# Backward of a recurrent-memory transformer on one core: the three projections of dH summed in one PSUM bank, in pairs of heads with 256 weight columns

## The chip, the cores and the metric

The kernel runs on one core of one Trainium2 chip. The metric is the device time of one execution in microseconds; three executions of the kernel before gave 3080.75, 3083.49 and 3086.59 us, median 3083.49. A core has a matrix engine (TensorE, "PE" in the profile, its weight loads "PEld"), a vector engine (DVE), a scalar engine (ACT), GpSimd (POOL), a queue engine (SP), and 16 DMA engines. PE reads two operands from SBUF, a stationary one (the weights in the array, loaded ahead) and a moving one that streams through, and writes PSUM, which has eight banks of 128 partitions by 512 float32 here. DVE and ACT bring results from PSUM to SBUF.

## What is computed

The reference is a block of adaLN conditioning, attention with a recurrent memory, and a gated feed-forward, with all its gradients. What matters here is the attention's backward pass. The forward pass goes over 64 segments of 32 tokens in order; each sees 8 memory rows and its own rows, and its first 8 output rows are the next segment's memory:

```python
h = jnp.concatenate([mem, xs], axis=1)          # (1, 8 + 32, 512)
q = jnp.einsum('btd,dhe->bhte', h, Wq)          # 32 heads of 128
k = jnp.einsum('btd,dhe->bhte', h, Wk)
v = jnp.einsum('btd,dhe->bhte', h, Wv)
...
o = jnp.einsum('bhte,hed->btd', o, Wo)
mem = o[:, :M, :].copy()
```

Backward therefore goes over the segments from the last to the first, and each one needs the gradient of its first 8 output rows from the one before it. That gradient is part of dH, the gradient of `h`:

dH = sum over heads of (dQ_h Wq_h^T + dK_h Wk_h^T + dV_h Wv_h^T),

a sum of 96 products of a 40x128 by a 128x512 matrix per segment. The 32 columns that hold the memory rows and the first 24 tokens are computed inside the loop; the last 8 tokens of each segment (its tail) are gathered over four segments and computed as one set of 32.

## The kernel before, in words

`phase4` is the backward loop, `for s in reversed(range(NS))` (L1560) with NS = 64. Its instructions are pinned on every engine in the order in which the Python code issues them (`self.pin(i0)`, L1755), so the code's order is each engine's order. Per segment it takes the gradient of the output rows, `dyT`, through Wo (`col_pass`, tile `pass_ps`), turns it per head (`turn`), and makes dV, dP, dS, dK and dQ in three parts of 12, 12 and 8 heads (`grad_mm`, `grad_out`, `dp`, `ds`, `dstt`). The gradients come out as `dVT`, `dKT` and `dQT`, with the head's 128 channels on the partitions and 32 columns for the rows of each head.

**The dH products.** With `X` (one of the three gradients) as the stationary operand, 128 by 32, a product fills 32 of the array's 128 columns. Four such products stand side by side in four column strips (`tile_position=(0, 32 * j)`) and write 32 partitions of the bank each.

- `dht` (L1641) does dV and dK with `col_mm` (L212): head n goes to strip n % 4, with all 512 weight columns moving. Each strip sums a quarter of the heads, so the bank `dh_ps`, 128 by 512, holds four partial sums of the whole 32x512 result. dV's first 24 heads come early (L1686, L1687), while the scores' gradient is made on DVE; dK's 32 heads and dV's last 8 come at L1722 to L1724.
- `dht_pairs` (L1649) does dQ with `pair_mm` (L218): two heads at a time, four products. Strips 0 and 1 take weight columns 0 to 255 of the two heads, strips 2 and 3 columns 256 to 511 of the same two. The bank `dhq_ps`, 128 by 256, holds two partial sums of each half.

**The split and the fold.** The partial sums are added on PE, by products with 0/1 matrices. To lose no precision in bf16, a bank is split in two parts, `hi` (ACT, a copy in bf16) and `lo` (DVE, bank less `hi`). `fold_split` (L307) does it for `dh_ps`, 128 by 512, into the tile of `dST`; `split_pair` (L226) for `dhq_ps`, 128 by 256, into `dh_hi` and `dh_lo`. `fold_sum` (L316) then makes 16 products of 32 columns into one bank `dh_ft`: eight with `foldsel` (adds four strips) on the first split, eight with `foldhalf` (adds two strips) on the second. `sum_pair` (L235), with the eight of the second kind alone, is what forward uses for its output projection.

**What lies around it.** Between the end of the dQ products and the fold stand, on PE, a piece of the tail's products (`tail.chunk()`, L1728; the pieces have 16, 24, 8, 8, 16, 8 and 16 products of 512 columns and are handed out over four segments) and, once in four segments, the tail's own fold (`self.pop_later()`, L1730, tile `dh_b_ft`). After the fold ACT brings the first 8 columns of `dh_ft` into the next segment's `dyT` (L1734), and PE goes on with a pass for the tails, `proj_b` (L1483), a turn of it, or another tail piece, and then with the next segment's `col_pass` on `dyT`.

**PSUM.** `psp` has six banks that are handed out in turn (tag "p": `pass_ps`, `turn_ps`, `g_ps`, `dp_ps`, `dhq_ps`, `dh_ft` and so on). `psb` has one bank for the tail (tag "b") and one, tag "dh", that `dh_ps` and `proj_b`'s `pass_ps` share.

**Queues.** SP issues the loads of the saved forward tiles and the two transposing DMAs of dK and dQ; POOL issues the stores, copies `dOst` and gathers the tails.

Of the kernel before, what the change touches and what calls it, by code (L numbers as in the profile page):

```python
# [8 lines left out]
F32 = mybir.dt.float32  # L9
# [31 lines left out]
class K:  # L41
# [1356 lines left out]
    def phase4(self):  # L1398
        nc, tc, cfg, io = self.nc, self.tc, self.cfg, self.io
        D, DC, H, E, L, M, T, G, NS = cfg.D, cfg.DC, cfg.H, cfg.E, cfg.L, cfg.M, cfg.T, cfg.G, cfg.NS  # L1400
        GW = 128
# [4 lines left out]
        with self.p4_ctx as ctx:  # L1406
            WqT, WkT, WvT, WoT, negones = self.WqT, self.WkT, self.WvT, self.WoT, self.negones
# [4 lines left out]
            sb2 = ctx.enter_context(tc.tile_pool(name="p4s2", bufs=2, reuse_waits="tile"))  # L1412
            psp = ctx.enter_context(tc.tile_pool(name="p4ps", bufs=6, space=PSUM, reuse_waits="tile"))
            psb = ctx.enter_context(tc.tile_pool(name="p4psb", bufs=1, space=PSUM, reuse_waits="tile"))
            NP = 3
            PG = 4
# [136 lines left out]
            def store_rows_x(left):  # L1553
                while len(row_stores) > left:
                    row_stores.pop(0)()
# [4 lines left out]
            for s in reversed(range(NS)):  # L1560
# [12 lines left out]
                dS, dST, dOst = dSs[0], dSTs[0], dOst_t  # L1573
                dVT, dKT, dQT = dXTs["dVT"][0], dXTs["dKT"][0], dXTs["dQT"][0]
# [63 lines left out]
                dh_ps = [None]  # L1638
                n_dh = [0]

                def dht(X, WT, pi):  # L1641
                    if dh_ps[0] is None:
                        dh_ps[0] = psb.tile([128, 512], F32, name="dh_ps", tag="dh")
                    for h in range(pi * PG * 3, min(H, (pi + 1) * PG * 3)):
                        off = (h // 3) * GW + (h % 3) * 32
                        self.col_mm(dh_ps[0], X[:, off:off + 32], WT[:, h, :], n_dh[0], 2 * H)
                        n_dh[0] += 1

                def dht_pairs(X, WT):  # L1649
                    ps = psp.tile([128, 256], F32, name="dhq_ps", tag="p")  # L1650
                    off = lambda h: (h // 3) * GW + (h % 3) * 32
                    for n in range(H // 2):
                        hs = (2 * n, 2 * n + 1)
                        self.pair_mm(ps, [X[:, off(h):off(h) + 32] for h in hs], [WT[:, h, :] for h in hs], n, H // 2)
                    return ps

                for a, n, eng in ((0, 4, "dve"), (4, 2, "act"), (6, 2, "act")):
                    self.col_pass(psp, WoT, 0, lambda c: dyT[:, c, :], RAd, eng, steps=(a, n))
# [25 lines left out]
                ds(2)  # L1684
                self.pop_later()
                dht(dVT, WvT, 0)  # L1686
                dht(dVT, WvT, 1)  # L1687
                gv2 = grad_mm("dVT", dOst, Pst, 2)
                gr0 = grad_mm("dV", Pst, dOst, 0)
# [32 lines left out]
                for pi in range(NP):  # L1722
                    dht(dKT, WkT, pi)
                dht(dVT, WvT, 2)  # L1724
                parts = self.fold_split(sb2, dh_ps[0], "dh", dST)
                pair = self.split_pair(sb2, dht_pairs(dQT, WqT), "dh")
                tail.collect(s % nseg_t, [dVT, dKT, dQT])
                tail.chunk()  # L1728
                if split:
                    self.pop_later()  # L1730
                store_rows_x(2)
                ft = self.fold_sum(psp, parts, "dh", "p", pair)
                if dyT_next is not None:
                    nc.scalar.activation(dyT_next[:, :, 0:M], ft[:, :, 0:M], AF.Copy)  # L1734
                g = s // 4
# [428 lines left out]
```

## Time and profile before

| | |
|---|---|
| median of three executions | 3083.49 us (3080.75 to 3086.59) |
| the profiled execution, its own time | 3080.64 us |
| its span, first to last instruction | 3078.9 us |
| PE busy | 2985.9 us, 97% |
| DVE, ACT, POOL busy | 1613.0, 1254.4, 1386.1 us |
| mean granted PE clock | 0.991 |
| first and last `dhq_ps` product | 1546.7 and 2501.3 us |

How to read the lines: a group is "line engine operation out<-in shapes xcount | busy us, mean ns of one | idle time before it". Busy time of a group is a union, so products that overlap are counted once. A line number can be a helper's: L215 is `col_mm`, L223 `pair_mm`, L255 `col_pass`, L323 `fold_sum`, L240 `sum_pair`. In a timeline a line starts with the moment and the duration of a run of equal instructions. A matmul's end is modelled, and the next one starts long before it, so the distance from one line's start to the next line's is what a run costs. A bracket at the end of a line names an idle time of the engine and who ended it. In the list of waits the three numbers are the total in us, how often, and the longest.

### The profile page before, as it was taken

Reading aid. Unit: us, or ns where it says so; the run is one execution under the profiler, and the core shown is the slowest. Engines: PE = TensorE matmul, PEld = TensorE weight load, DVE = VectorE, ACT = ScalarE, POOL = GpSimd, SP = SyncE. Lnnn points to the kernel's source line nnn. Section 1 sums busy time; section 2 is a strip of 40 time slices with the busy share of each in tenths; the row PEclk is TensorE's granted clock in tenths of the full one; section 3 lists DMA queues with packets and bytes.
Section 4 is the critical chain, followed back from the end, with each engine's and each line's share of the span. In section 5 each row is a group of like instructions: output and inputs, shape, how many; then the busy total and the mean of one; then the engine's idle time right before and its main releaser. Section 6 shows DMA issues by size and latency. Waiting matters only on the chain.

```text
span 3078.9 us, 106050 instructions
## 1 busy us (share of the span) xinstructions
PE 2985.9 (97%) x43769; PEld 1821.5 (59%) x43845; DVE 1613.0 (52%) x3799; ACT 1254.4 (41%) x3056; POOL 1386.1 (45%) x2960
## 2 busy tenths in 40 slices
PE   6999999999999799989899999999999999999999
PEld 3666666666665444445577777777777754445455
DVE  4556656665655788742255555555555632322221
ACT  2555555555555433322155555555555520111011
POOL 3666767667766222211244444444444422333322
PEclk8999999999999899999999999999999999999999
DMA  8888788788778799997599999999999998666574
GB/s 300 217 215 204 204 209 217 203 214 212 206 202 255 199 229 231 225 282 254 176 232 246 244 247 246 245 248 244 248 243 245 253 278 278 201 194 221 188 236 149
DMA packets 845992, 703.54 MB, mean 229 GB/s; under 512 B 544354, under 2 KB 717954, under 8 KB 845124
## 3 DMA queue, kind: packets, MB, share of 16 engines
q1 hardware_dynamic: 714196, 486.69, 62.7%
q0 software_dynamic: 60656, 148.64, 15.1%
q10 hardware_dynamic: 70656, 61.41, 6.4%
q8 instruction: 345, 5.65, 0.8%
q14 instruction: 139, 1.14, 0.1%
HBM read 294.93 MB, written 276.35 MB: 186 GB/s over the span
## 4 chain that ended last, share of the span: by engine, by line
PE 45%; issue 3%; POOL 1%; DMA 1%; DVE 0%; ACT 0%; SPq 0%; POOLq 0%
PE gps L1954 9%; PE dh_ps L215 8%; PE g_ps L1616 6%; PE pass_ps L255 5%; PE gps5o L1968 5%; PE dhq_ps L223 4%; PE dh_tps L215 3%; PE dp_ps L1593 2%; PE tps L1526 2%; PE dp_ps L1601 1%; PE turn_ps L1480 1%; PE dh_ft L323 1%; POOL out_dram L1958 1%; DMA dhb<-DHA 0%; PE turn_ps L264 0%
## 5 line engine op out<-in xcount | busy, mean ns | idle before, releaser
L1954 PE MATMUL gps<-rows,hrows 128*128 128x512 bf16 (+2 forms) x2124 | 415.6, 355 | 1.9
L1954 PEld LDWEIGHTS <-hrows 128*128 128x128 bf16 x2160 | 211.3, 98 | 204.5
L255 PEld LDWEIGHTS <-hT 128*32 128x32 bf16 x6144 | 158.3, 97 | 168.5 <-DMA Wq<-in_A_Wq_dram 5.5
L1660 POOL COPY dOst<-RAd 96x512 bf16<-96x512 bf16 x128 | 75.5, 613 | 311.4 <-DVE RAd L63 311.2
L63 DVE CAST ot<-gps 128x512 bf16<-128x512 f32 (+3 forms) x76 | 48.1, 633 | 286.9 <-PE gps L1954 188.4
L1958 POOL DMA_DIRECT2D out_dram<-ot x108 | 81.5, 755 | 255.9 <-DVE ot L63 137.2
L61 ACT ACTIVATE ot<-gps 128x512 bf16<-128x512 f32 (+3 forms) x75 | 41.3, 551 | 352.3 <-PE gps L1954 230.7
L909 POOL TENSOR_TENSOR Pst<-Pst,rden 120x1408 bf16<-120x1408 bf16 x63 | 159.7, 2536 | 47.7 <-issue 21.4
L61 ACT ACTIVATE dVT<-g_ps 128x480 bf16<-128x480 f32 (+1 forms) x192 | 104.7, 545 | 95.5 <-PE g_ps L1616 95.1
L63 DVE CAST RA0v<-pass_ps 128x512 bf16<-128x512 f32 x128 | 88.5, 692 | 91.2 <-PE pass_ps L255 85.3
L255 PE MATMUL pass_ps<-Wv,hT 128*32 128x512 bf16 x2048 | 134.2, 382 | 0.0
L215 PE MATMUL dh_ps<-WvT,dVT 128*32 128x512 bf16 x2048 | 133.4, 380 | 0.3 <-DVE RBd L63 0.2
L255 PE MATMUL pass_ps<-Wq,hT 128*32 128x512 bf16 x2048 | 123.3, 383 | 5.3 <-DMA Wq<-in_A_Wq_dram 5.3
L1968 PE MATMUL gps5o<-WoT,rows 128*128 128x512 bf16 x580 | 127.7, 379 | 0.6
L223 PE MATMUL at_ps<-Wo,OT 128*32 128x256 bf16 x4096 | 124.6, 274 | 3.0 <-DMA Wo<-in_A_Wo_dram 3.0
L255 PE MATMUL pass_ps<-Wk,hT 128*32 128x512 bf16 x2048 | 121.6, 379 | 2.2 <-ACT hT L899 1.1
L255 PE MATMUL pass_ps<-WoT,dyT 128*32 128x256 bf16 (+1 forms) x3072 | 122.4, 308 | 0.9 <-ACT dyT L1734 0.9
L223 PE MATMUL dhq_ps<-WqT,dQT 128*32 128x256 bf16 x4096 | 122.9, 273 | 0.0
L215 PE MATMUL dh_ps<-WkT,dKT 128*32 128x512 bf16 x2048 | 122.3, 380 | 0.0
L223 PEld LDWEIGHTS <-dQT 128*32 128x32 bf16 x4096 | 109.6, 97 | 15.9
L1603 DVE SCALAR_TENSOR_TENSOR dS<-dp_ps,Pst_l 128x480 bf16<-128x480 f32 (+1 forms) x192 | 106.1, 608 | 19.2 <-PE dp_ps L1601 19.2
L223 PEld LDWEIGHTS <-OT 128*32 128x32 bf16 x4096 | 103.8, 97 | 18.6 <-issue 6.5
(421 smaller groups left out, 7034.9 us busy)
## 6 DMA issues: line engine op xcount, KB each, us to landing
OSR<-Ost SPq DMA_DIRECT2D x64, 352.0 KB
OT<-OT SPq DMA_DIRECT2D x64, 352.0 KB
VT<-VTr SPq DMA_DIRECT2D x64, 352.0 KB
PS<-Pst SPq DMA_DIRECT2D x64, 352.0 KB
OT_l<-OT SPq DMA_DIRECT2D x64, 352.0 KB
Pst_l<-PS SPq DMA_DIRECT2D x64, 352.0 KB
VT_l<-VT SPq DMA_DIRECT2D x64, 352.0 KB
DVR<-rows_x POOLq DMA_DIRECT2D x64, 352.0 KB, 6.2
```

Of the source, the lines that this page charges most:

```text
L61: return nc.scalar.activation(out, in_, AF.Copy)
L63: return nc.vector.tensor_copy(out, in_)
L215: self.nc.tensor.matmul(ps[32 * j:32 * j + 32, :], lhsT=lhsT, rhs=w, start=(n < 4), stop=(n >= total - 4), tile_position=(0, 32 * j))
L223: nc.tensor.matmul(ps[32 * j:32 * j + 32, :], lhsT=x[k], rhs=w[k][:, 256 * d:256 * d + 256], start=(n == 0), stop=(n == total - 1), tile_p ...
L255: self.nc.tensor.matmul(ps[32 * j:32 * j + 32, :], lhsT=lhs(c), rhs=rhs, start=(c == 0), stop=(c == DC - 1), tile_position=(0, 32 * j))
L909: nc.gpsimd.tensor_tensor(Pst[0:120, :, :], Pst[0:120, :, :], rden[:, :].unsqueeze(2).to_broadcast([120, G, 128]), op=ALU.mult)
L1603: nc.vector.scalar_tensor_tensor(out=part3(dS, pi)[:, :, 0:120], in0=ps[:, 0:n, 0:120], scalar=cfg.scale, in1=part3(Pst, pi)[:, :, 0:120], ...
L1616: nc.tensor.matmul(ps[:, j, 0:w], lhsT=lh[:, g * GW:(g + 1) * GW], rhs=rh[:, g * GW:g * GW + w], start=True, stop=True)
L1660: nc.gpsimd.tensor_copy(dOst[0:96, 512 * hf:512 * hf + 512], RAd[0:96, 512 * hf:512 * hf + 512])
L1954: nc.tensor.matmul(ps[:, 0:ng * E], lhsT=hrows[:, tp_, c * 128:(c + 1) * 128], rhs=rows[:, tp_, 0:ng * E], start=(tp_ == 0), stop=(tp_ == ...
L1958: nc.gpsimd.dma_start(outw[c * 128:(c + 1) * 128, h0:h0 + 3 * (ng - 1) + 1:3, :], ot[:, 0:ng * E].rearrange("p (h e) -> p h e", e=E))
L1968: nc.tensor.matmul(pss[gg][:], lhsT=src[0][:, src[1], gg * E:(gg + 1) * E], rhs=dyrows[:, tp_, :], start=(tp_ == order[0]), stop=(tp_ == o ...
```

## The change

dV's and dK's parts go through `pair_mm`, as dQ's did, into the same bank as dQ's. `dh_ps` is the first half of a bank (128 by 256); the 96 heads' products are 48 pairs, 192 products of 256 columns, with one start and one end of the accumulation. `dht_pairs` and the bank `dhq_ps` go. One `split_pair` follows dQ's last product, and `sum_pair` folds with eight products instead of sixteen. `fold_split` and `fold_sum` stay for the tail alone. The places at which dV's, dK's and dQ's products are issued stay the same.

```diff
                 def dht(X, WT, pi):
                     if dh_ps[0] is None:
-                        dh_ps[0] = psb.tile([128, 512], F32, name="dh_ps", tag="dh")
-                    for h in range(pi * PG * 3, min(H, (pi + 1) * PG * 3)):
-                        off = (h // 3) * GW + (h % 3) * 32
-                        self.col_mm(dh_ps[0], X[:, off:off + 32], WT[:, h, :], n_dh[0], 2 * H)
+                        dh_ps[0] = psb.tile([128, 512], F32, name="dh_ps", tag="dh")[:, 0:256]
+                    off = lambda h: (h // 3) * GW + (h % 3) * 32
+                    for n in range(pi * PG * 3 // 2, min(H, (pi + 1) * PG * 3) // 2):
+                        hs = (2 * n, 2 * n + 1)
+                        self.pair_mm(dh_ps[0], [X[:, off(h):off(h) + 32] for h in hs], [WT[:, h, :] for h in hs],
+                                     n_dh[0], 3 * H // 2)
                         n_dh[0] += 1
-
-                def dht_pairs(X, WT):
-                    ps = psp.tile([128, 256], F32, name="dhq_ps", tag="p")
-                    off = lambda h: (h // 3) * GW + (h % 3) * 32
-                    for n in range(H // 2):
-                        hs = (2 * n, 2 * n + 1)
-                        self.pair_mm(ps, [X[:, off(h):off(h) + 32] for h in hs], [WT[:, h, :] for h in hs], n, H // 2)
-                    return ps
...
                 for pi in range(NP):
                     dht(dKT, WkT, pi)
                 dht(dVT, WvT, 2)
-                parts = self.fold_split(sb2, dh_ps[0], "dh", dST)
-                pair = self.split_pair(sb2, dht_pairs(dQT, WqT), "dh")
+                for pi in range(NP):
+                    dht(dQT, WqT, pi)
+                parts = self.split_pair(sb2, dh_ps[0], "dh")
                 tail.collect(s % nseg_t, [dVT, dKT, dQT])
                 tail.chunk()
                 if split:
                     self.pop_later()
                 store_rows_x(2)
-                ft = self.fold_sum(psp, parts, "dh", "p", pair)
+                ft = self.sum_pair(psp, parts, "dh", "p")
```

## The prediction

> **What bounds the kernel now.** I read the page first, then PE's waits inside the backward loop, then the busy time of that stretch, then PE's timeline over a few segments, and last the two evacuations that feed the fold.
>
> ```profile
> PE 2985.9 (97%) x43769; PEld 1821.5 (59%) x43845; DVE 1613.0 (52%) x3799; ACT 1254.4 (41%) x3056; POOL 1386.1 (45%) x2960
> L223 PE MATMUL dhq_ps<-WqT,dQT 128*32 128x256 bf16 x4096 | 122.9, 273 | 0.0
> L215 PE MATMUL dh_ps<-WkT,dKT 128*32 128x512 bf16 x2048 | 122.3, 380 | 0.0
> ```
> PE is the bound of the whole program. The two groups below it do the same amount of work in the two shapes that the change exchanges: 32 heads in 64 segments, once as 4096 products of 256 columns, once as 2048 of 512. They cost 122.9 and 122.3 us.
>
> PE's waits from 1540 to 2500 us, which is the backward loop:
> ```profile
> PE pass_ps L255 <- ACT dyT L1734: 0.9, 3, 0.3
> PE dh_ft L323 <- ACT dh_hi L230: 0.8, 4, 0.2
> PE dh_ft L323 <- DVE dh_lo L232: 0.8, 4, 0.2
> ```
> Busy time in the steady part of it (PE, PEld, DVE, ACT, POOL, granted clock, DMA share, GB/s):
> ```profile
> 1700.00:2500.00 800.00, 798.25 (x16690) 570.55 (x16690) 465.35 (x1175) 424.41 (x1097) 370.57 (x917) 1.00 0.99 248
> ```
> PE waits for nothing in the steady loop (the four waits on `dh_hi` and `dh_lo` belong to the first four segments), and its clock is at 1.00. So a segment lasts as long as PE's stream, and work taken from that stream shortens the segment if no wait opens in its place. DVE and ACT are half idle; what they are relieved of is worth nothing by itself. The DMA share of 0.99 is packets in flight. PE waits for no transfer in this stretch, and a segment that is 0.12 us of 15 shorter asks for 1% more, so I cost that at nothing.
>
> PE's timeline, one segment with tail products (start, duration):
> ```profile
> 2013.01 1.91 PE L215 MATMUL dh_ps<-WkT,dKT 128*32 128x512 bf16 x32
> 2014.74 0.60 PE L215 MATMUL dh_ps<-WvT,dVT 128*32 128x512 bf16 x8
> 2015.17 1.92 PE L223 MATMUL dhq_ps<-WqT,dQT 128*32 128x256 bf16 x64
> 2016.92 1.04 PE L215 MATMUL dh_tps<-WqT,dh_tail 128*32 128x512 bf16 x16
> 2017.89 0.37 PE L323 MATMUL dh_ft<-foldsel,dST 128*128 128x32 bf16 x8
> 2018.11 0.25 PE L323 MATMUL dh_ft<-foldsel,dh_hi 128*128 128x32 bf16 x4
> 2018.21 0.25 PE L323 MATMUL dh_ft<-foldsel,dh_lo 128*128 128x32 bf16 x4
> 2018.39 0.62 PE L255 MATMUL pass_ps<-WoT,dyb 128*32 128x512 bf16 x8
> ```
> ACT's and DVE's part of it, from the timeline of all engines:
> ```profile
> 2017.15 0.38 ACT L230 ACTIVATE dh_hi<-dhq_ps 128x256 bf16<-128x256 f32 x1 [1.09 <-PE dhq_ps L223]
> 2017.57 0.43 DVE L232 TENSOR_TENSOR dh_lo<-dhq_ps,dh_hi 128x256 bf16<-128x256 f32 x1 [0.78 <-ACT dh_hi L230]
> ```
> And a segment without tail products ahead of the fold (the second of the loop):
> ```profile
> 1561.61 1.92 PE L223 MATMUL dhq_ps<-WqT,dQT 128*32 128x256 bf16 x64
> 1563.46 0.36 PE L323 MATMUL dh_ft<-foldsel,dST 128*128 128x32 bf16 x8
> 1564.02 0.27 PE L323 MATMUL dh_ft<-foldsel,dh_hi 128*128 128x32 bf16 x4 [0.19 <-ACT dh_hi L230]
> 1564.48 0.27 PE L323 MATMUL dh_ft<-foldsel,dh_lo 128*128 128x32 bf16 x4 [0.19 <-DVE dh_lo L232]
> ```
> The starts, not the durations, give the cost, since products overlap. I count from T0, the moment at which the last dQ product has been issued: 2016.92 above, and 1561.61 + 1.75 = 1563.36 here.
>
> **The change part by part.**
>
> *Products of 512 columns become twice as many of 256.* Four of them, one per column strip, run side by side. From the starts: 40 products of 512 take 2015.17 - 2013.01 = 2.16 us, 0.216 per four; 64 of 256 take 2016.92 - 2015.17 = 1.75 us, 0.109 per four. A segment has 64 of the first kind for dV and dK, 16 fours; they become 32 fours of 0.109. Difference: 16 x (2 x 0.1094 - 0.216) = 0.045 us; the page's busy totals (122.9 against 122.3 us per 32 heads) give 2 x 0.6 / 64 = 0.02. I take 0.04, nearer the timeline, because busy totals include overlaps with the neighbours. Leaving the strips for a full-width product is unchanged: after 256 columns the first fold product comes 1563.46 - 1561.61 - 1.75 = 0.10 us behind the end of the stream, after 512 it is 2017.89 - 2016.92 - 4 x 0.216 = 0.11. Over 64 segments: +2.6 us.
>
> The trace has the 256-column fours at 0.109 us and the 512-column fours at 0.216. The Trainium skill, "TensorE: Matmul & The Clock Gate", section "Back-to-back issue gap", gives N/2.4 + 2.5 ns, a fixed part per product, which speaks against this change: 2 x 109.2 - 215.8 = 2.6 ns per pair. By it this term would be 16 x 2.6 ns x 64 = 2.7 us, an estimate from that page, so rule and rows lead to the same sum.
>
> *Eight of the sixteen fold products go* (L323, `dh_ft<-foldsel,dST`). Four fold products are 0.10 us apart from the next four (2018.11 to 2018.21), so eight are 0.20; the other 0.02 of the 0.22 at 2017.89 is the first one's start, which the `dh_hi` products inherit. What is late next is `dh_lo`. Its chain starts with the last dQ product, as before: where PE waits for it, in the second segment, `dh_hi` is used at T0 + 0.66 and `dh_lo` at T0 + 1.12. The fold without the eight would start at T0 + 0.97 in the segment above (16 tail products), so `dh_hi` is there and costs no wait; the `dh_lo` products would follow at T0 + 1.085 but can only start at T0 + 1.12. With the wider spacing after a wait (the four `dh_lo` products take 0.27 us there against 0.25) that takes back 0.05: saving 0.15 us.
>
> Which segments: the tail pieces are (16, 24, 8, 8, 16, 8, 16) products, handed out in that order over s%4 = 3, 2, 2, 1, 1, 0, 0. Ahead of the fold lie 16 (s%4 = 3, plus the eight `dh_b_ft` products, 0.2 us), 24 (s%4 = 2), 16 and 16. So for s%4 = 3 and 2 the fold starts 0.2 and 0.43 us later than in the segment shown, `dh_lo` is there in time, and the full 0.20 is saved. For s%4 = 1 and 0 it is 0.15. The first four segments (s = 63 to 60) have no tail piece and wait for `dh_hi` and `dh_lo` today; the eight products lie inside those waits, so nothing is saved there. Sum: 30 x 0.20 + 30 x 0.15 = 10.5 us.
>
> Bounds of this term: from above, 60 x 0.22 = 13.2; from below, nothing where `dh_lo` is close, if PE resumes much later than the second segment shows: 30 x 0.20 = 6.0.
>
> *One evacuation pair goes* (ACT L312 0.60 us, DVE L313 0.69 us per segment, 64 times 128x512). Neither is on the path: both end before T0 (ACT 2015.46 to 2016.06, DVE 2016.09 to 2016.78), and the second pair waits for dQ, not for them. Worth nothing. `dST` also is free earlier, but its next writer comes half a segment later.
>
> *The bank.* `dh_ps` is now held until `dh_lo` has been made instead of until L313, about 1.2 us longer. Its next user is `proj_b`'s pass over `dyb` (2018.39), which stands behind the `dh_lo` products on PE and so waits already. The rotation of six banks loses one request per segment, which only makes the others older when they are reused. Nothing.
>
> *Order on the queues.* No DMA, no instruction on POOL or SP is added, removed or moved; PE gets 64 products and 64 weight loads more in the places of the old ones, less 8 + 8 of the fold. Nothing is queued behind a new wait but the fold itself and what follows it at the same distance: ACT's `dyT` evacuation and the next pass.
>
> **Sum.** -10.5 + 2.6 = -7.9 us in 64 segments, about 0.12 us of 15. The stage behind the loop is PE's as well (no transfer ended a wait of PE after 2480 us), so it only starts earlier. The profiled execution took 3080.64 us (span 3078.9), which makes 3072.7; it lies 2.85 below the median of the three runs, 3083.49, and against that the forecast is 3075.6 us, -0.26%. A measurement of this kernel tells about 0.2%, 6.2 us, from no change.
>
> **The rivals.**
> 1. *The wait gives half of it back.* The fold gets shorter but PE stands at `dh_lo` until the old time in every segment with s%4 = 1 or 0. For it: only 0.03 to 0.05 us lie between the two moments. Against it: the second segment shows T0 + 1.12, and the first `dh_lo` product today starts at T0 + 1.29. Price: -6.0 + 2.6 = -3.4, 3080.1 us, the same within the bound.
> 2. *It does not do what it says.* The removed products were filling time that PE would spend anyway, in all segments: +2.6, 3086.1 us. It needs a wait today that the eight products hide with 16 to 24 tail products ahead; the waits of PE show such a thing in four segments of 64.
> 3. *Slower: PE runs out of instructions.* The narrow products double the rate at which PE takes instructions, and the dense stretch grows from 64 products to 144 (dK, the rest of dV, dQ). The instruction queue in the steady part (packets, MB, share of 16 engines over 800 us):
> ```profile
> q8 instruction: 131, 2.15, 1.2%
> ```
> That is a block per 6.1 us, and 2 x 16690 / 131 = 255 of PE's instructions in each, and 0.012 x 16 x 800 / 131 = 1.2 us for one to arrive. At 128 instructions in 1.75 us a block lasts 3.5 us, three times its transfer. If nevertheless one transfer a segment were exposed: 64 x 1.2 = 75 us, 3151 us; it decides from 0.22 us per segment, (7.9 + 6.2) / 64, or 7 ns per four. Against it: forward's and backward's 64-product stretches run at 0.109 us to the end.
> The Trainium skill, "Runtime: NRT & Kernel Launch", section "Instruction fetch mechanics", says that the sequencer fetches the next block of 256 instructions while it executes the current one; no run here shows how far ahead.
>
> **How the numbers follow.** Forecast 0.62, rival 1 0.20, rival 2 0.07, rival 3 0.11. The chance of faster is the forecast's; same is rivals 1 and 2, 0.27; slower is rival 3. Range: low, 60 x 0.22 - 64 x 0.02 = 11.9 saved, 3071.6, and 2.7 for the spread of the runs (3080.75 is that far below the median): 3069. High: rival 1 at 3080.1 and rival 2 at 3086.1, of which I take in most: 3085. That leaves out rival 3 and some of rival 2 and of the low end.
>
> **What would show it.** Right: `dh_ps` at 256 columns 192 products per segment at 0.109 us per four (about 368 us for all 12288 in union); no `foldsel,dST` group; fold from its first product to the next pass about 0.35 us where s%4 = 1 or 0 and 0.30 elsewhere, against 0.50; a short new wait of PE or its weight loads on `dh_lo`; the loop's four-segment period 60.64 us becoming some 60.1. Wrong: fours above 0.112 us, gaps inside the dense stretch with nothing waited for, a wait for `dh_lo` of 0.2 us, or a wait on a transfer that the trace of before does not have.

## The result

The changed kernel takes 3119.5 us (median of four executions, 3110.78 to 3128.61), against 3082.12 us for the kernel before on the same chip (four executions, 3080.61 to 3086.59). The ratio is 1.0119, 95% interval [1.0086, 1.0152]: slower by 1.2%, where 0.26% faster was forecast. The profiled execution took 3116.11 us, with a span of 3114.3.

### The profile page after: what moved, and what is told of

Read it like the earlier page. It is cut to its first block, busy times and chain, and to the rows that moved or that the text cites. A ratio compares the mean times of both kernels' runs of the same rounds, so it can differ in the third digit from the quotient of the medians.

```text
span 3114.3 us, 113509 instructions
## 1 busy us (share of the span) xinstructions
PE 2999.5 (96%) x47429; PEld 1922.1 (62%) x47429; DVE 1569.0 (50%) x3735; ACT 1217.1 (39%) x2992; POOL 1391.5 (45%) x2960
## 4 chain that ended last, share of the span: by engine, by line
PE 44%; issue 4%; POOL 1%; DMA 1%; ACT 0%; DVE 0%; SPq 0%; POOLq 0%; ACTq 0%
PE dh_ps L223 11%; PE gps L1949 9%; PE g_ps L1616 6%; PE pass_ps L255 5%; PE gps5o L1963 4%; PE dh_tps L215 3%; PE dp_ps L1593 2%; PE tps L1526 2%; PE dp_ps L1601 1%; PE turn_ps L1480 1%; POOL out_dram L1953 1%; PE dh_ft L240 1%; DMA rows<-DVR 0%; PE turn_ps L264 0%; DMA dhb<-DHB 0%
## 5 line engine op out<-in xcount | busy, mean ns | idle before, releaser
L232 DVE TENSOR_TENSOR dh_lo<-dh_ps,dh_hi 128x256 bf16<-128x256 f32 x64 | 27.2, 425 | 247.8 <-ACT dh_hi L230 247.8
L223 PE MATMUL dh_ps<-WvT,dVT 128*32 128x256 bf16 x4096 | 137.0, 274 | 1.3 <-issue 1.2
L223 PE MATMUL dh_ps<-WqT,dQT 128*32 128x256 bf16 x4096 | 126.5, 273 | 10.7 <-issue 10.6
L223 PE MATMUL dh_ps<-WkT,dKT 128*32 128x256 bf16 x4096 | 124.5, 273 | 1.3 <-issue 1.1
```

The lines of the kernel that those rows point to most:

```text
L223: nc.tensor.matmul(ps[32 * j:32 * j + 32, :], lhsT=x[k], rhs=w[k][:, 256 * d:256 * d + 256], start=(n == 0), stop=(n == total - 1), tile_p ...
```

## The profile after

The page of the changed kernel: PE's totals, the instruction queue over the whole span, and the three groups of dH products (busy time and mean duration, then the idle time ahead and what ended most of it).

```profile
PE 2999.5 (96%) x47429; PEld 1922.1 (62%) x47429; DVE 1569.0 (50%) x3735; ACT 1217.1 (39%) x2992; POOL 1391.5 (45%) x2960
q8 instruction: 373, 6.11, 0.8%
L223 PE MATMUL dh_ps<-WvT,dVT 128*32 128x256 bf16 x4096 | 137.0, 274 | 1.3 <-issue 1.2
L223 PE MATMUL dh_ps<-WqT,dQT 128*32 128x256 bf16 x4096 | 126.5, 273 | 10.7 <-issue 10.6
L223 PE MATMUL dh_ps<-WkT,dKT 128*32 128x256 bf16 x4096 | 124.5, 273 | 1.3 <-issue 1.1
```

The products themselves cost what was forecast, 273 ns each, and the `foldsel,dST` group is gone. New are the idle times ahead of them, which end with "issue": PE waited for nothing that the profile shows. The instruction queue brings PE's own instructions: 373 packets of 16 KB.

PE's waits from 1540 to 2500 us (total, how often, longest):

```profile
PE dh_ps L223 <- issue: 12.1, 15, 1.5
PE dh_tps L215 <- issue: 4.5, 9, 1.0
PE dh_ft L240 <- ACT dh_hi L230: 2.0, 4, 0.5
PE dh_ft L240 <- DVE dh_lo L232: 0.8, 4, 0.2
```

The two waits on the split are those of the first four segments and no others; the first two lines had no counterpart before. The list holds only the part of a stop that the modelled matmul ends do not cover. Below I count stops from start to start instead: a gap of over 0.33 us between the starts of two successive PE instructions, less the 0.06 us that lie between them anyway.

The steady part of the loop (PE, PEld, DVE, ACT, POOL, granted clock, DMA share, GB/s):

```profile
1700.00:2500.00 800.00, 777.63 (x19032) 632.65 (x19030) 415.91 (x1086) 382.32 (x1012) 363.77 (x897) 1.00 0.98 238
```

PE is busy for 777.63 us of 800, where it was 798.25. The clock is as before. PE takes 47.6 instructions a microsecond (products and loads together) where it took 41.7.

One segment with a stop in it, from PE's timeline (start, duration):

```profile
1807.93 1.93 PE L223 MATMUL dh_ps<-WkT,dKT 128*32 128x256 bf16 x64
1809.69 0.61 PE L223 MATMUL dh_ps<-WvT,dVT 128*32 128x256 bf16 x16
1810.12 1.58 PE L223 MATMUL dh_ps<-WqT,dQT 128*32 128x256 bf16 x50
1813.21 0.61 PE L223 MATMUL dh_ps<-WqT,dQT 128*32 128x256 bf16 x14 [1.50 <-issue]
1813.55 1.13 PE L215 MATMUL dh_tps<-WvT,dh_tail 128*32 128x512 bf16 x16
1814.42 0.70 PE L215 MATMUL dh_tps<-WkT,dh_tail 128*32 128x512 bf16 x8
1815.05 0.26 PE L240 MATMUL dh_ft<-foldsel,dh_hi 128*128 128x32 bf16 x4
1815.16 0.25 PE L240 MATMUL dh_ft<-foldsel,dh_lo 128*128 128x32 bf16 x4
1815.35 0.61 PE L215 MATMUL dh_tps<-WkT,dh_tail 128*32 128x512 bf16 x8
```

The 64 products of dK take 1809.69 - 1807.93 = 1.76 us, 0.110 per four, and the fold from its first product to what follows it 0.30 us. In between, in the middle of dQ's products, PE stands still for 1.5 us, though ACT had written the last of `dQT` by 1808.97 us.

**Where the time came from.** The loop, from the first dV product to the last `dh_ft` product, took 962.5 us before and takes 996.9: +34.4. What follows the loop is the same (576.1 and 576.6). Inside it:

- Stops at one place of PE's instruction order. Of 61 gaps over 0.33 us in the loop, 44 end at the same position modulo 256 when PE's products, weight loads and semaphore instructions are counted through, and they make 35.2 us. (The semaphore instructions, four per segment, have to be counted: with products and loads alone no position has more than three gaps.) The instruction queue's packets are blocks of 16 KB, one for each 256 of PE's instructions (a block, below); in the loop exactly one packet starts between the beginning of a block and that of the next. Each of these stops ends 1.2 to 1.8 us after such a packet has landed. From the first instruction of a block to the moment at which PE goes on with the next one it takes 3.7 to 6.9 us, median 5.2, in these 44 cases: 2.6 until a packet starts, 1.1 for the packet, 1.4 from its landing until PE goes on.
- Segments without a stop. Their four-segment period was 60.64 us and is 60.34, so 16 times -0.30 = -4.8 us. The forecast was -0.54 at this place; the rest is an added 0.06 us per segment, told below.
- The remaining +4.0 us are what is left of the difference. Smaller gaps and waits such as `g_ps <- POOL dOst` (1.2 us) are candidates; I did not assign them one by one.

256 successive PE instructions took at least 4.71 us anywhere in the loop of the kernel before, median 6.08. In the changed kernel they take as little as 3.40, and 18% of all such stretches are below 4.5 us. The dense blocks are not the only ones that stop, though: 17 of these stops end blocks that had themselves run for over 4.7 us.

## The experiments

Each was compared with runs of the kernel before on its own chip. The expectations use letters. A is the theory that PE runs out of instructions where 256 of them go by faster than the next block arrives. B, the first rival, is that the narrow products do no harm and the loss lies in what was merged: the common bank, the one split, the shorter fold. Later A1 stands for a block that is late because the loop's own transfers are ahead of it, A2 for a fetch that takes its time whatever else is being moved.

| run | median us | ratio to before [95%] | loop us | stops at block boundaries |
|---|---|---|---|---|
| before | 3082.12 | 1 | 962.5 | none |
| after | 3119.5 | 1.0119 [1.0086, 1.0152] | 996.9 | 44, 35.2 us |
| e1_halves | 3156.9 | 1.0236 [1.0221, 1.0251] | 1039.8 | 70, 73.4 us |
| e2_fold8 | 3076.42 | 0.9971 [0.9962, 0.9981] | 952.9 | none |
| e3_before_plain | 3147.31 | 1.0207 [1.0192, 1.0223] | 1026.9 | 12, 10.7 us |
| e4_after_plain | 3171.64 | 1.0287 [1.0270, 1.0304] | 1053.0 | 41, 43.7 us |
| e6_dk_halves | 3097.79 | 1.0047 [1.0032, 1.0062] | 980.7 | 20, 16.7 us |
| e7_after_pass44 | 3127.76 | 1.0151 [1.0131, 1.0170] | 1003.5 | 39, 36.1 us |
| e8_before_copy | 3084.63 | 1.0001 [0.9992, 1.0011] | 965.2 | none |
| e9_after_copy | 3107.18 | 1.0078 [1.0063, 1.0093] | 990.0 | 29, 27.3 us |
| e10_before_light | 3081.57 | 0.9991 [0.9982, 1.0001] | 963.3 | none |
| e11_after_light | 3079.26 | 0.9985 [0.9976, 0.9995] | 960.7 | 2, 1.3 us |
| e12_after_late | 3137.59 | 1.0185 [1.0161, 1.0209] | 1016.4 | 58, 53.6 us |
| e13_after_later | 3157.3 | 1.0239 [1.0213, 1.0264] | 1039.4 | 77, 73.5 us |

### e1: the narrow products alone

The kernel before, with each of dV's and dK's products cut in two of 256 columns that go to the same strip and bank as before. The bank of 512, both splits, both evacuation pairs and all 16 fold products stay.

```diff
-                        self.col_mm(dh_ps[0], X[:, off:off + 32], WT[:, h, :], n_dh[0], 2 * H)
+                        for d in range(2):
+                            for j in range(4):
+                                off = ((h0 + j) // 3) * GW + ((h0 + j) % 3) * 32
+                                nc.tensor.matmul(dh_ps[0][32 * j:32 * j + 32, 256 * d:256 * d + 256],
+                                                 lhsT=X[:, off:off + 32], rhs=WT[:, h0 + j, 256 * d:256 * d + 256],
...
```

> The kernel before, with dV's and dK's products cut into two of 256 columns each, into the same 512-column bank and the same strips. Both splits, both banks and all sixteen fold products stay. Theory A (PE runs out of instructions: 64 products and 64 weight loads more per segment, the same dense stretch of 144 products as in the changed kernel): 2.6 us for the narrower fours plus stalls as in the changed kernel's loop (some 37 us, each ended 1.2 to 1.6 us after a block of instructions had landed), 3115 to 3130 us. Theory B (the narrow products are harmless; the loss comes from the one bank, the single split and the wait for dh_lo in the shorter fold): 2.6 us, 3084 to 3086 us, and no gaps without a releaser in the dense stretch.

Measured: 3156.9 us, 73 us above the kernel before. PE's waits in the loop (1540 to 2500 us) are of the same kind as in the changed kernel, only more of them:

```profile
PE dhq_ps L223 <- issue: 28.4, 25, 1.9
PE dh_tps L215 <- issue: 10.7, 13, 1.6
```

And its timeline shows two stops in one segment:

```profile
2114.90 0.40 PE L1649 MATMUL dh_ps<-WkT,dKT 128*32 128x256 bf16 x8
2116.08 1.71 PE L1649 MATMUL dh_ps<-WkT,dKT 128*32 128x256 bf16 x56 [0.78 <-issue]
2117.62 0.61 PE L1649 MATMUL dh_ps<-WvT,dVT 128*32 128x256 bf16 x16
2118.05 1.70 PE L223 MATMUL dhq_ps<-WqT,dQT 128*32 128x256 bf16 x56
2120.92 0.40 PE L223 MATMUL dhq_ps<-WqT,dQT 128*32 128x256 bf16 x8 [1.16 <-issue]
```

Between the two stops lie 56 + 16 + 56 = 128 products with 128 loads, one block of 256; its products started within 3.4 us, and the next block went on 2120.92 - 2116.08 = 4.84 us after this one. B falls: none of what it names is in this kernel, and the loss is twice that of the changed one. A stands; the size was beyond what I had expected of it (31 to 46 us). The changed kernel loses less than e1, though its narrow products are the same. e1 also holds the eight fold products and the wider splits. Why that makes twice the stops was not separated.

### e2: the fold's eight products alone

The kernel before, without the eight `foldsel,dST` products, so that dV's and dK's share of dH is missing from the result.

```diff
-                ft = self.fold_sum(psp, parts, "dh", "p", pair)
+                ft = self.sum_pair(psp, pair, "dh", "p")
```

> The kernel before, with the eight fold products of dV's and dK's split left out (their share of dH is missing from the result; the split itself stays). This is the saving of the change without its narrow products. Theory A: 8 x 25 ns less in the 60 segments that have tail products ahead of the fold, 0.20 us each, 0.15 where dh_lo is close: 10 us less, 3070 to 3074 us. Theory B: PE stands at dh_lo for as long as the eight products took, in half of the segments or in all: 3076 to 3083 us, with waits of 0.1 to 0.2 us on dh_lo in each.

Measured: 3076.42 us, ratio 0.9971; the loop is 9.6 us shorter, with no stops. The four segments of a period got shorter by 0.146, 0.145, 0.199 and 0.200 us. The timeline of one of them, with the fold from 2017.47 to 2017.82, 0.35 us:

```profile
2014.76 1.92 PE L223 MATMUL dhq_ps<-WqT,dQT 128*32 128x256 bf16 x64
2016.50 1.04 PE L215 MATMUL dh_tps<-WqT,dh_tail 128*32 128x512 bf16 x16
2017.47 0.27 PE L240 MATMUL dh_ft<-foldsel,dh_hi 128*128 128x32 bf16 x4
2017.63 0.27 PE L240 MATMUL dh_ft<-foldsel,dh_lo 128*128 128x32 bf16 x4
2017.82 0.61 PE L255 MATMUL pass_ps<-WoT,dyb 128*32 128x512 bf16 x8
```

The prediction's largest term, 0.20 and 0.15 us, is right to 0.005 us. The whole program gained less than the loop, 7.6 us against 3084.04 on the same chip, which puts the time 2.4 us above A's range and into B's; but B's waits on `dh_lo` are not there (four, in the first four segments), so the loop decides for A. The gain is there, and in the changed kernel it is paid away by the stops.

### e6: dK's products alone

As e1, for dK's 32 products only, so that the dense stretch holds 64 + 64 narrow products with dV's eight wide ones between them.

```diff
+                    if X is dKT:
+                        hs = range(pi * PG * 3, min(H, (pi + 1) * PG * 3))
...
```

> The kernel before, with dK's 32 products alone cut in two of 256 columns (same bank, same strips), dV's left at 512; half of the extra instructions of the run that cut both. Theory A (a block of 256 instructions has to last longer than its fetch, some 4.2 to 5.3 us from one block's beginning to the next one's arrival; cutting both made 256 instructions take as little as 3.4 us): about half of that run's 73 us or less, since the stretch of dK, dV's rest and dQ holds 136 products instead of 144 but the segment's average falls from 48 to 45 instructions per us: 20 to 45 us, 3104 to 3129 us. Theory B (narrow products are harmless): 1.3 us, 3085 us.

Measured: 3097.79 us, 13.6 above before. Of the stops 20 are at block boundaries, 16.7 us; a period without one is only 4 x 0.02 us longer. PE's waits in the loop:

```profile
PE dh_tps L215 <- issue: 4.5, 7, 1.3
PE dhq_ps L223 <- issue: 2.3, 2, 1.2
```

The direction is A's, the size below what I expected of it. The densest 256 instructions take 3.61 us here and 17% of the stretches are below 4.5, as in the changed kernel; so the density of the stretch alone doesn't fix how often PE stops. What is being moved when a block is fetched was the next suspect, and the next runs went for that.

### e3 and e4: no transposing transfers (a base with a loss of its own)

dK's and dQ's gradients are stored as they lie, by direct stores, in the kernel before (e3) and in the changed one (e4).

```diff
-                        rows = rxp.tile([128, G, 128], BF16, name="rows_x")
-                        nc.sync.dma_start(rows[:], xt[:, :], transpose=True)
...
-                        row_stores.append(lambda: nc.gpsimd.dma_start(dram, rows[:]))
+                        row_stores.append(lambda: nc.gpsimd.dma_start(dram, gl3(xt)))
```

> The kernel before, with dK's and dQ's gradients stored as they lie, by the same stores, without the two transposing DMAs per segment (the weight gradients made from them are not the right ones). It is the base for the next run. PE waits for no transfer in the loop, so all theories expect 3079 to 3084 us.

> The changed kernel with the same left out: no transposing DMAs of dK and dQ in the loop. Theory A1 (blocks of instructions come late because they queue behind the loop's DMA traffic, the transposes above all): the stalls go, and what is left is the undisturbed period of four segments, 60.34 us against 60.64, so 5 us below the kernel before without transposes: 3074 to 3080 us. Theory A2 (73 instructions per us is more than the instruction queue can deliver, whatever else runs): still 30 to 40 us above it, 3110 to 3125 us. Theory B: as A2, but with waits that have a releaser on ACT or DVE.

Measured: 3147.31 and 3171.64 us. e3 is 2% slower than the kernel before, for reasons of its own. Its list of waits in the loop (1540 to 2550 us) begins with these:

```profile
PE dhq_ps L223 <- ACT dQT L61: 31.9, 59, 1.6
PE pass_ps L255 <- issue: 4.0, 4, 1.7
```

The first line is half of e3's 63 us: the gradients' tiles are held until the stores are through, so the next segment's evacuations wait. With that in nearly every segment the totals can't answer the question, and e4's 24 us above e3 are no verdict.

The stops of the two runs do say something. e4 has no transposing transfers, a DMA share of 0.60, and 41 stops of 43.7 us, more than the changed kernel with them; so A1 does not hold in the form "the transposes above all". And e3, whose products of dV and dK are the wide ones and whose densest 256 instructions take 4.64 us, has 12 stops at block boundaries, 10.7 us. The blocks ahead of them had run for 4.9 to 5.7 us, and the next packet had started only 3.2 to 4.4 us after their beginning (median 3.6). A dense stretch is therefore not needed for a stop, where the fetch starts late enough.

### e8 and e9: the transposing transfers as plain copies

The same two transfers into the same tiles, as copies that don't transpose, in the kernel before (e8) and in the changed one (e9).

```diff
-                        nc.sync.dma_start(rows[:], xt[:, :], transpose=True)
+                        nc.sync.dma_start(rows[:], gl3(xt))
```

> The kernel before, with the two transposing DMAs of dK and dQ per segment replaced by plain copies into the same tiles (the weight gradients made from them are not the right ones). Same tiles, waits and stores, unlike the run that stored directly and so made PE wait for the stores. Base for the next run; PE waits for no transfer today, so 3079 to 3086 us.

> The changed kernel with the same plain copies. Theory A1 (the fetch is slow because its packets queue behind the transposes): the stalls go and it is 4 to 6 us below the kernel before with copies. Theory A2 (the fetch takes 4 to 5 us with or without the transposes): 25 to 40 us above it, as with them. In between: the transposes are a part of the queue.

Measured: e8 takes 3084.63 us, as before; e9 3107.18, 22.6 above e8, where the unedited pair is 37 apart. The window from 1700 to 2480 us of e9, in which the DMA share is 0.75 with the bytes as they were:

```profile
1700.00:2480.00 780.00, 762.92 (x18722) 620.15 (x18714) 406.53 (x1062) 373.13 (x989) 354.73 (x878) 1.00 0.75 240
```

Stops fall from 35.2 to 27.3 us. That lies between A1 and A2, nearer to A2's 25 us, and decides nothing: there is an effect of the traffic, but a base was needed with much less of it.

### e10 and e11: much less traffic

As e8 and e9, and besides the four loads of saved forward tiles are cut: `Pst` and `VT` are loaded once for all segments, `Qst` and `Kst` are not loaded again. The instructions of PE, DVE and ACT stay those of the two kernels.

```diff
+                    if not once:
+                        for nm, dram in (("Pst", self.PS), ("VT", self.VT)):
...
-                load_rows(Qst_t, self.QST, s - 1)
...
-                    if pi == NP - 1:
-                        load_rows(Kst_t, self.KST, s - 1)
```

> The kernel before with plain copies for the two transposing DMAs, and with Pst, VT, Qst and Kst loaded once for the last segment and kept (four of the loop's five loads of some 340 KB per segment are left out; the gradients of all other segments are made from the wrong tiles). Base for the next run; PE waited for no transfer before, so 3079 to 3087 us.

> The changed kernel with the same left out. With the copies alone it was 22.6 us above its base, and a block of instructions that PE stood waiting for came 5.2 us after the beginning of the block before it (median), of which 2.4 us until its packet started, 1.3 for the packet, 1.5 until PE went on. Theory A1 (the 2.4 us are the queue of the loop's other transfers): with 40% of the bytes gone they shrink, blocks come in under 4 us, and most stalls go: 5 us below to 10 above the base. Theory A2 (the fetch takes this long by itself): 20 to 37 us above the base.

Measured: 3081.57 us for e10 and 3079.26 for e11. The windows of the two (e10 first), same columns as above:

```profile
1700.00:2480.00 780.00, 778.75 (x16293) 557.54 (x16286) 455.11 (x1150) 413.53 (x1069) 361.39 (x901) 1.00 0.45 153
```

```profile
1700.00:2480.00 780.00, 778.37 (x19240) 639.48 (x19229) 419.67 (x1099) 383.55 (x1019) 362.70 (x896) 1.00 0.45 155
```

PE's waits of e11 in the loop:

```profile
PE dh_ft L240 <- ACT dh_hi L230: 2.0, 4, 0.5
PE pass_ps L255 <- ACT dyT L1731: 0.9, 3, 0.3
PE dh_ft L240 <- DVE dh_lo L232: 0.8, 4, 0.2
PE dh_ps L223 <- issue: 0.3, 1, 0.3
```

PE takes 49.3 instructions a microsecond in e11, more than in the changed kernel, and is busy for all but 1.6 us of 780. The same dense stretches pass without stops once the DMA share is 0.45: two are left, 1.3 us. From the beginning of a block to the next instruction packet it is 0.95 us at the median, against 1.70 in e9 and 2.22 in the changed kernel (over all blocks, those without a stop too); the packet itself takes 1.0 to 1.1 us in all three. So the changed kernel's loss needs both, its dense stretches and the loop's traffic, and A2 falls: what makes a block late is that its packet starts late, and that goes with what the loop moves. The mean DMA share alone does not order the runs, though: e4 at 0.60 has more stops than e9 at 0.75. Without the stops the changed kernel's loop is 2.6 us shorter than its counterpart, and the totals are 0.9985 [0.9976, 0.9995] and 0.9991 [0.9982, 1.0001] of before, which this measurement does not tell apart.

### e7: fewer products elsewhere

The changed kernel with `dyT`'s pass in two steps instead of three, 4 and 4 chunks, which takes 16 products and 16 loads a segment out of a place that isn't dense.

```diff
-                for a, n, eng in ((0, 4, "dve"), (4, 2, "act"), (6, 2, "act")):
+                for a, n, eng in ((0, 4, "dve"), (4, 4, "act")):
```

> The changed kernel with the pass over dyT in two blocks of 512 columns instead of one of 512 and two of 256: 16 products and 16 weight loads fewer per segment, the same work, one ACT evacuation of 512 columns instead of two of 256. Theory A: fewer instructions, so fewer and shorter stalls: 5 to 20 us below the changed kernel, 3100 to 3114 us; of this the later evacuation may take back up to 0.2 us a segment, 13 us. Theory B: no gain, 0 to 13 us above the changed kernel.

Measured: 3127.76 us, 8 above the changed kernel's median of 3119.5 (on another chip, where before took 2.1 us longer), a difference inside the changed kernel's own spread and in the range given for B. The stops are what they were, 36.1 us; the densest 256 instructions are still 3.40 us. So these 32 instructions a segment, taken from another place, bought nothing. The loop is 6.5 us longer; four segments without a stop take some 0.39 us more, 6.2 us in 16 such periods. The later evacuation, which the expectation priced at up to 13 us, is there: the eight `turn_ps` products of a segment take 0.175 us longer. Part of that is made good behind them; where was not settled.

### e12 and e13: the loads in another place

The changed kernel with the loads of `Qst` and `Kst` moved on SP behind the two transposing transfers, in the hope that the dense stretch would meet a shorter queue (e12); and in addition dQ's store issued earlier, beside dK's at the segment's beginning (e13).

```diff
-                load_rows(Qst_t, self.QST, s - 1)
...
-                    if pi == NP - 1:
-                        load_rows(Kst_t, self.KST, s - 1)
...
+                load_rows(Qst_t, self.QST, s - 1)
+                load_rows(Kst_t, self.KST, s - 1)
                 tail.collect(s % nseg_t, [dVT, dKT, dQT])
```

```diff
-                store_rows_x(1)
+                store_rows_x(0)
```

> The changed kernel, whole, with the loads of the next segment's Qst and Kst issued on SP behind both transposing DMAs, after the dense stretch of PE's products, instead of ahead of them. Theory A1 (a block of instructions queues behind the transfers that are under way in the dense stretch): two of 340 KB less there, so fewer stalls: 5 to 25 us below the changed kernel, 3094 to 3114 us; without any stall it would be 3079 to 3081. Against it: the dQ transpose then starts earlier in the stretch. If the loads come late for their products, a wait of PE on a transfer shows.

> As the run before it, and DQR's store issued with DKR's at the segment's beginning instead of just ahead of the dense stretch. Theory A1: another 352 KB less in the stretch, 3 to 10 us below the run before it; if the store has to wait for the transposed rows, POOL's copies behind it come late and PE waits for them.

Measured: 3137.59 and 3157.3 us, 18 and 38 above the changed kernel where a gain was expected. PE's waits of e12 in the loop (1540 to 2500 us):

```profile
PE dh_ps L223 <- issue: 13.5, 20, 1.9
PE g_ps L1616 <- issue: 13.2, 11, 2.7
PE tps L1526 <- issue: 4.1, 2, 2.6
PE pass_ps L255 <- issue: 2.9, 4, 1.8
```

The stops in dQ's products did not go, and new, longer ones stand in the next segment's products (`g_ps`, `tps`), where there had been almost none: 0.9 us in three waits for `g_ps` in the changed kernel. In the stops, from a block's beginning until PE goes on it is now 6.3 us at the median and 9.0 at most, against 5.2 and 6.9; the difference is in the time until the packet starts, 3.6 us against 2.6. The same bytes, later and closer together, hold up the blocks longer. That the order of the loop's transfers moves the stops by tens of microseconds is shown; which transfer a block stands behind is not.

## Why the prediction was wrong, point by point

- *The narrow products, +0.04 us per segment.* Right. In segments without a stop dV's and dK's stretches are 0.039 us longer together, and a four takes 0.110 us.
- *Eight fold products, -0.20 and -0.15 us.* Right, by e2: -0.20 and -0.145. The split's moments are as worked out: in the second segment, where PE waits, the `dh_hi` products start at T0 + 0.66 and the `dh_lo` products at T0 + 1.12, with the last dQ product issued at 1562.81 + 1.75 = 1564.56:

```profile
1562.81 1.92 PE L223 MATMUL dh_ps<-WqT,dQT 128*32 128x256 bf16 x64
1565.22 0.27 PE L240 MATMUL dh_ft<-foldsel,dh_hi 128*128 128x32 bf16 x4 [0.49 <-ACT dh_hi L230]
1565.68 0.27 PE L240 MATMUL dh_ft<-foldsel,dh_lo 128*128 128x32 bf16 x4 [0.20 <-DVE dh_lo L232]
```

- *The evacuation pair worth nothing; the bank held longer, no wait.* Nothing speaks against either: ACT and DVE were relieved by some 40 us each, PE has no wait for the bank of `dh_ps`.
- *"No DMA ... is added" and the queues at nothing.* Wrong by what I did not count there. PE's instructions are themselves brought by DMA: 28 more blocks (373 against 345).
- *Missing term, +0.06 us per segment.* From the first `tps<-ident,dS` product to the first `g_ps<-dS,Qst` product it takes 0.655 us where it took 0.596, because the latter waits for ACT's evacuation of an older bank (`rows_x<-g_ps`): it starts 0.05 us after that evacuation's end in both kernels, and the evacuation is 0.06 us later. In 64 segments 3.8 us, half of the forecast gain. With e2's -0.69 per period, +0.16 for the narrow products and +0.24 for this, the sum is -0.29; measured -0.30. I had written that losing one request in the rotation of six banks only makes the others older. It is in the changed kernel and in its variants e7, e9 and e11, and not in e1, e2 and e6. ACT's evacuation of the `dVT` bank ahead of it is already late, 0.43 us after its last three products begin instead of 0.37. As e1 has the narrow products of dV too, their width alone is not the reason. Which other part of the change delays it stays open.
- *Rival 3, "PE runs out of instructions".* This is what happened, and the sign that was named for it came, gaps inside the dense stretch with nothing waited for. The step that failed is its dismissal: "At 128 instructions in 1.75 us a block lasts 3.5 us, three times its transfer." The 3.5 us were right (3.40 measured). The transfer's 1.2 us were not what to compare with: a packet's own duration is one term of three, and the whole way in the 44 stops was 5.2 us at the median, 2.6 before the packet starts, 1.1 for it and 1.4 after it has landed. A block of 3.4 us is short against that, not three times as long. The second argument, that forward's and backward's 64-product stretches ran without gaps, showed nothing of 144: 64 products are half a block, and the densest 256 instructions in the backward loop before took 4.71 us (5.09 in forward), and no stop came of it there. The rival's price, one transfer per segment or 75 us, was twice what came: 44 stops of 0.8 us.
- *The DMA share of 0.99.* I set it aside because PE waited for no transfer. The traffic behind it was the other half of the cause (e10 and e11), though the share by itself is a poor measure of it (e4 against e9).

The Trainium skill, "Runtime: NRT & Kernel Launch", section "Instruction fetch mechanics", says that the sequencer fetches the next page while it executes the current one and that crossing a 16 KiB boundary is mostly hidden. That agrees with the kernel before and with e11; with PE at 75 instructions a microsecond (256 in 3.40 us) under a DMA share of 0.98 it was not hidden, 35.2 us in the changed kernel, nor in e3, 10.7 us.

## What to carry to other kernels

Before cutting a dense stretch of matmuls into smaller ones, count products, loads and semaphore instructions together over any 256 in a row, and compare the time of the densest such stretch with the densest that already runs without "issue" gaps under the same traffic: below that, nothing in the profile of before vouches for the instruction supply. That is a warning and not a threshold: e3 stopped at blocks of 4.9 us and more, when the transfers lay otherwise. A packet's duration is not its latency; the time until it starts counts. A stop that the profile gives to "issue", and that comes back at one position modulo 256 in that count, is this one, and much less traffic in the loop or a less dense stretch are what made it go here; issuing the same loads later and closer together made it worse.

## What the runs showed that I had not expected

- How far apart the parts of a fetch lie: 2.6 us until the packet starts, 1.1 us for 16 KB, and another 1.4 us from landing until PE goes on.
- Traffic that no engine waits for can still set the pace: the next packet started 0.95 us after a block's beginning in e11 (DMA share 0.45) and 2.22 us after it in the changed kernel (0.98; medians).
- After one of the stops, at 1593.2 us, the granted clock fell for some microseconds. The windows of the changed kernel there, the clock in the third column from the end:

```profile
1590.00:1593.00 3.00, 3.00 (x108) 2.83 (x110) 0.91 (x2) 1.26 (x3) 3.00 (x7) 1.00 1.07 407
1593.00:1595.00 2.00, 0.55 (x23) 0.26 (x15) 0.00 (x0) 0.00 (x0) 0.92 (x3) 1.00 1.10 266
1595.00:1598.00 3.00, 2.35 (x49) 1.44 (x53) 0.84 (x2) 0.58 (x2) 0.00 (x0) 0.77 1.46 160
```

  From 1700 to 2500 us, with most of the stops in it, the mean is 1.00; so this is not where the time went.
